# A gated attention and its feed-forward network on one core: the range check of the weights done by VectorE late, instead of by ScalarE throughout

## The chip, the cores and the metric

The kernel runs on one core of a Trainium2 chip. Times are device microseconds (us) of one execution. Five executions of the kernel before took 573.87 to 575.8 us, with a median of 574.09 us. One more execution was recorded by the hardware profiler, and all lines shown from the trace are of that one.

## The reference

Four batches, eight heads, 768 tokens, 48 features a head. A complex gate per token and feature is first brought to a magnitude of at most 0.999; a state is then carried over the tokens, and its real part is read by the queries. The result, 3072 rows of 384, goes through a feed-forward network (FFN):

```
mag = np.sqrt(a_re * a_re + a_im * a_im)
scale = np.minimum(mag, 0.999) / (mag + 1e-06)
...
new_re = ar * S_re - ai * S_im
new_im = ar * S_im + ai * S_re
S_re, S_im = (new_re + kv, new_im)
y[:, :, t] = np.einsum('bhd,bhde->bhe', q[:, :, t], S_re)
...
a = x @ w1
b = x @ w2
h = a * b @ w3
return (h @ w_out).astype(np.float32)
```

w1 and w2 are 384x1024, w3 is 1024x1024, w_out is 1024x384. The four weights arrive as 64-bit floats, all else as 32-bit floats.

## The kernel before, in words

**Work.** The tokens are cut into eight units (u = 0 to 7), two for each batch, of 384 tokens each. For a unit the kernel prepares the gates (`gates(u)`), then does the attention in three chunks of 128 tokens, then the FFN of the unit. The product of w3 and w_out is formed once, at the start (L940), so that an FFN has only two stages. In `ffn_ab` (L714 to L729), for each of eight blocks j of 128 hidden features, TensorE multiplies with w1 and then with w2 into two PSUM buffers (L723), ScalarE copies the first out (L728), and VectorE multiplies the second by that copy (L729, tile `ab`). In `out_pair` and `ffn_out`, TensorE multiplies `ab` by the fused weight (L768, L802). The `mm` PSUM pool has four buffers, so block j+2 can write its second product only when VectorE's product of block j is done.

**Gates.** `gates(u)` is a chain that goes to and fro between ScalarE (logarithm, exponential, arc tangent, sine, all at L544) and VectorE (products and scans, L554 to L620). The gates of unit u+1 are prepared while unit u is worked on. The first TensorE instruction of a unit that needs them is the transpose `tp` of the tile gR (L653); gR is finished by VectorE at L616, tile k at L617.

**The range check.** The kernel's fast way holds only for inputs in a certain range. While it runs, it collects evidence that they are: `check_gates` looks at the gates, and `check_weights` at the weights. Where the evidence is bad, the function `general` computes all again (L1084 to L1086); here it does not. `check_weights` is a generator. Each step loads one piece of a weight (a DMA from SyncE's queue, called SP, into one of two buffers `look`, 512 KB or, for w_out, 384 KB), as pairs of 32-bit words, and looks at the high words of the 64-bit numbers read as 32-bit floats. There are 36 such looks: 28 of 512 numbers a partition, 8 of 384. A look is two ScalarE passes, for the 16 pieces of w3 three: the square of the scaled high word, in place (L885), then Relu with a sum (L886) that is over zero when a number is too small, and for w3 another (L888) that is over zero when one is too large. The sums lie in `st_wts`. `judge` (L946) turns all evidence into counts, adds them over the partitions with one small TensorE product (`count`, L961), and sets the flag `good`. Every engine reads the flag at the end.

**What sets the order.** TensorE's instructions run in the order of the program text (`manual_schedule`, L1009). On the other engines, and in SP's queue, a scheduler orders the instructions when the program is built; `high_priority` lifts some of them, and `follow` (L861) keeps a look behind the last instruction in `copied`. The order is then fixed: each engine, and SP, takes its instructions in turn, and one that waits holds all behind it. `unit` (L993) emits a unit's pieces and takes one look at each of its 10 or 11 places i, for units 2 to 7. After the last unit, the rest of the looks and `judge` are emitted (L1077 to L1079), and then the last FFN, of unit 7, by which the kernel ends.

Of the kernel before, what the change touches and what calls it, by code (L numbers as in the profile page):

```python
# [10 lines left out]
FP = mybir.dt.float32  # L11
I32 = mybir.dt.int32
# [3 lines left out]
AF = mybir.ActivationFunctionType  # L16
# [358 lines left out]
def kernel(  # L375
# [36 lines left out]
    nc = tc.nc  # L412
# [16 lines left out]
    LO, HI = 32, D - 32  # L429
    LN_EPS = math.log(1e-6)  # L430
    PI = math.pi
    MIN_SQ, MAX_SQ = 1.126 ** 2, 2.0 ** 32 - 512
    SMALL, LARGE, STEEP, DECAY, ANGLE = 2.0 ** -7, 2.0 ** 40, 1.5, math.exp(-64.0), 50.0

    weights_pool = ctx.enter_context(tc.tile_pool(name="weights", bufs=1))
# [24 lines left out]
    causal = singles.tile([P, C], I32, name="causal")  # L460
    nc.gpsimd.iota(causal, pattern=[[1, C]], base=0, channel_multiplier=-1)
    nc.vector.tensor_scalar(out=causal, in0=causal, scalar1=0, scalar2=None, op0=OP.is_ge)
    consts = singles.tile([P, 7], FP, name="consts")
    for i, x in enumerate((1.0, LN_EPS, PI / 2, SMALL, -LARGE, MIN_SQ, -MAX_SQ)):
        nc.vector.memset(consts[:, i:i + 1], x)
    ONE, EPS, QUARTER, LEAST, MOST, TINY, TWO = (consts[:, i:i + 1] for i in range(7))

# [2 lines left out]
    nc.vector.memset(st_tan, 0.0)  # L472
    nc.vector.memset(st_low, 0.0)

    st_wts = singles.tile([P, 80], FP, name="st_wts")
    nc.vector.memset(st_wts, 0.0)
    st_dec = singles.tile([P, NU, KD], FP, name="st_dec")
    st_ang = singles.tile([P, NU, KD, UC], FP, name="st_ang")

# [236 lines left out]
    def ffn_ab(u, j):  # L716
        if j == 0:
            ab_t[u] = one.tile([P, KF, TT], FP, tag="ab", name="ab")
        got = []
        for w in (w1s, w2s):  # L720
            m = ps_m.tile([P, TT], FP, tag="mm", name="m")
            for f in range(KD):
                nc.tensor.matmul(out=m, lhsT=w[:, j * P // WB, f, j * P % WB:j * P % WB + P], rhs=xT_t[u][:, f],  # L723
                                 start=(f == 0), stop=(f == KD - 1))
            got.append(m)
        a = two.tile([P, TT], FP, tag="a", name="a")
        with tc.high_priority():
            copied[:] = [nc.scalar.copy(out=a, in_=got[0])]  # L728
            nc.vector.tensor_tensor(out=ab_t[u][:, j], in0=got[1], in1=a, op=OP.mult)  # L729

# [128 lines left out]
    def follow(work):  # L861

        for ins in work:
            tc.add_manual_dep(ins.ins, copied[-1].ins.name, ORDER, reason="later")

    def check_weights(late):

        for u in range(2):
            for f in range(KD):
                re = late.tile([P, 2, TT], FP, tag="look", name="look")  # L870
                load_rows(re, art, u, [f])
                follow(check_gates(u, re[:, 0], re[:, 1], f))
                yield
        n = 0
        for w in (w1, w2, w3t, wo):
            if w.dtype == FP:
                continue
            src = words(w)
            step = min(src.shape[2], 1024)
            for i in range(src.shape[1]):  # L880
                for j in range(0, src.shape[2], step):
                    raw = late.tile([P, 512, 2], I32, tag="look", name="look")
                    nc.sync.dma_start(out=raw[:, 0:step // 2].rearrange("p m w -> p (m w)"), in_=src[:, i, j:j + step])
                    lo, hi = (raw[:, 0:step // 2, x].bitcast(FP) for x in range(2))
                    follow([nc.scalar.activation(out=hi, in_=hi, func=AF.Square, scale=2.0 ** 15)])  # L885
                    nc.scalar.activation(out=lo, in_=hi, func=AF.Relu, scale=-1.0, bias=TINY, accum_out=st_wts[:, n:n + 1])  # L886
                    if w is w3t:
                        nc.scalar.activation(out=hi, in_=hi, func=AF.Relu, bias=TWO, accum_out=st_wts[:, n + 40:n + 41])  # L888
                    n += 1
                    yield  # L890

# [54 lines left out]
    def judge():  # L946

        n = max(NU * KD * UC, st_wts.shape[1])
        ok = singles.tile([P, n], FP, name="ok")
        tot = singles.tile([P, 6], FP, name="tot")  # L950
        dec, ang = st_dec.rearrange("p u f -> p (u f)"), st_ang.rearrange("p u f c -> p (u f c)")
        low, tan = st_low.rearrange("p x u f -> p (x u f)"), st_tan.rearrange("p u f -> p (u f)")
        need = 0
        for i, (t, op, x) in enumerate(((dec, OP.is_ge, DECAY), (ang, OP.is_le, ANGLE), (ang, OP.is_ge, -ANGLE),
                                        (low, OP.is_le, 0.0), (tan, OP.is_le, STEEP * STEEP), (st_wts, OP.is_le, 0.0))):
            m = t.shape[1]
            need += m
            nc.vector.scalar_tensor_tensor(out=ok[:, 0:m], in0=t, scalar=x, in1=ONE.to_broadcast([P, m]), op0=op,
                                           op1=OP.mult, accum_out=tot[:, i:i + 1])
        m = ps_m.tile([P, TT], FP, tag="mm", name="count")  # L960
        nc.tensor.matmul(out=m[0:1, 0:6], lhsT=ONE, rhs=tot, start=True, stop=True)  # L961
        count = singles.tile([1, 7], FP, name="count")
        nc.vector.scalar_tensor_tensor(out=count[:, 0:6], in0=m[0:1, 0:6], scalar=1.0, in1=ONE[0:1].to_broadcast([1, 6]),
                                       op0=OP.mult, op1=OP.mult, accum_out=count[:, 6:7])
        nc.vector.tensor_scalar(out=good, in0=count[:, 6:7], scalar1=float(P * need), scalar2=None, op0=OP.is_equal)

    for A in Ab:
        nc.vector.memset(A, 0.0)
# [24 lines left out]
    def unit(u, steps, rest, look, ahead):  # L993

        for f in rest[:ahead]:
            f()
            next(steps, None)
        rest = rest[ahead:]
        p = pieces(u) + [[]]
        n = len(p)  # L1000
        first = [i * (len(rest) - 2) // (n - 1) for i in range(n)] + [len(rest)] if u > 1 else [0, 1, 1, 2, 2, 3, 3, 3, 4, 4, 6]
        for i in range(n):
            for f in rest[first[i]:first[i + 1]] + p[i]:
                f()
                next(steps, None)
            next(look, None)

    gate_pool[1] = fast.enter_context(tc.tile_pool(name="late_gates", bufs=1))
    with tc.manual_schedule(engines={mybir.EngineType.PE}):  # L1009

        phase = rounding()
        row_load(0, 4)
        load_gates(0)
        row_load(1)
        row_load(2)
        row_load(3)
        take_qk(0)
        steps = gates(0, True)
        for f in range(KF):
            row_work(f)  # L1020
            if f == 0:
                load_qkv(0)
            if f + 4 < KF:
                row_load(f + 4)
            if f >= KF - 2:
                continue
            for j in range(KF):
                fuse(f, j)
            for _ in range(2):
                next(steps, None)  # L1030
        work = w12_work()
        for f in work[:2]:
            f()
        for _ in steps:
            pass
        for f in range(KF - 2, KF):
            for j in range(KF // 2):
                fuse(f, j)
        fill = [lambda f=f, j=j: [fuse(f, j + x) for x in range(2)] for f in range(KF - 2, KF) for j in range(KF // 2, KF, 2)]
        load_gates(1)  # L1040
        steps = gates(1, False)
        take_qk(1)
        rest = ffn(0, 2)
        work = work[2:]
        for i, p in enumerate(pieces(0)):
            for f in p:
                f()
            if i in (1, 3, 6, 9):
                fill.pop(0)()
            if i == 0:  # L1050
                for f in work[:2]:
                    f()
                load_qkv(1)
            if i >= 2:
                next(steps)
            if i in (5, 7):
                work[2 + (i == 7)]()
        for i, f in enumerate(rest[:HEAD]):
            f()
            if i < 2:  # L1060
                work[4 + i]()
            if i == 2:
                phase.close()
            if i < 6:
                next(steps)
            if i == KF - 1:
                for _ in steps:
                    pass
        late = fast.enter_context(tc.tile_pool(name="late", bufs=1))
        look = check_weights(fast.enter_context(tc.tile_pool(name="looks", bufs=2)))  # L1070
        out_weights()
        for u in range(1, NU):
            steps = gates(u + 1, False) if u + 1 < NU else iter(())
            unit(u, steps, rest[HEAD:] if u == 1 else ffn(u - 1), look if u > 1 else iter(()), AHEAD[u])
            for _ in steps:
                pass
        for _ in look:  # L1077
            pass
        judge()  # L1079
        for f in ffn(NU - 1, 2):  # L1080
            f()
    fast.close()

    value = nc.values_load(good[0:1, 0:1], min_val=0, max_val=1)  # L1084
# [38 lines left out]
```

## Time and profile before

| | |
|---|---|
| median of five executions | 574.09 us |
| profiled execution | 573.73 us |
| its span, first to last instruction | 571.8 us |
| mean granted TensorE clock | 0.992 |
| TensorE matmuls (PE) busy | 545.4 us, 95% |
| VectorE (DVE) busy | 335.4 us, 59% |
| ScalarE (ACT) busy | 347.3 us, 61% |
| passes of the looks at the weights on ACT, first and last start | 207.1 and 448.6 us |
| attention of unit 7 and FFN of unit 6 | about 459 to 520 us |
| FFN of unit 7 | 520 us to the end |

The table is read from the top: the span is what the instructions take from first to last, and 1.9 us of the profiled execution lie around it. An engine that is busy 95% of the span leaves little room; engines busy 60% may still be late for it in some places. In a line of the trace, the first number is the start in us from the span's start, or the line group's count where it begins with a source line; "[1.42 <-DVE gR L616]" is idle time before an instruction and the instruction that ended it.

### The profile page before, as it was taken

What the parts mean: (1) busy time and instruction counts of PE and PEld (TensorE: products, weight loads), DVE (VectorE), ACT (ScalarE), POOL (GpSimd) and SP (SyncE); (2) the same over time, 40 slices, a digit from 0 to 9 for tenths busy, and PEclk for the clock granted to TensorE, in tenths of its full rate; (3) what the DMA queues carried; (4) which work ended last, traced back from release to release, by engine and by line L of the source; (5) the groups of instructions that cost most, each with busy time, mean ns of one, the idle gap of its engine ahead of it and who ended that gap; (6) DMA issues with size and microseconds to landing.
All of it is one profiled execution on the core that took longest, in us unless ns stands there. A gap on an engine that the chain in (4) does not pass through costs nothing.

```text
span 571.8 us, 9280 instructions
## 1 busy us (share of the span) xinstructions
PE 545.4 (95%) x3682; PEld 387.2 (68%) x3682; DVE 335.4 (59%) x507; ACT 347.3 (61%) x569; POOL 3.5 (1%) x9
## 2 busy tenths in 40 slices
PE   4779999999999999999999999999999999999995
PEld 2345775578556985688567975697567966796565
DVE  6898489946852577356752686355743696332121
ACT  6998668537572799459963898279964745101100
POOL 2000000000000000000000000000000000000000
PEclk9899999999999999999999999999999999999999
DMA  8994997393273345944593527844483103300001
GB/s 277 368 370 132 251 350 207 111 234 85 86 161 86 112 152 193 240 139 154 182 213 116 150 73 223 214 141 155 130 198 107 30 28 104 76 2 30 0 1 47
DMA packets 46340, 84.74 MB, mean 148 GB/s; under 512 B 4688, under 2 KB 36176, under 8 KB 45392
## 3 DMA queue, kind: packets, MB, share of 16 engines
q1 hardware_dynamic: 46288, 84.06, 50.6%
q8 instruction: 31, 0.51, 0.4%
q14 instruction: 21, 0.17, 0.1%
HBM read 60.42 MB, written 4.72 MB: 114 GB/s over the span
## 4 chain that ended last, share of the span: by engine, by line
PE 66%; DVE 12%; ACT 11%; DMA 6%; issue 3%; SPq 1%; DVEq 0%; ACTq 0%
PE m L723 36%; PE p L768 10%; PE o L802 6%; PE sc L665 4%; PE y L692 4%; PE kv L703 3%; ACT gZ L544 2%; DMA re<-in_a_re_dram 2%; ACT gR L544 2%; DVE gZ L600 2%; PE tp L653 2%; DMA raw<-in_w_dram 2%; DMA QL<-gA 1%; ACT re L544 1%; ACT gA L544 1%
## 5 line engine op out<-in xcount | busy, mean ns | idle before, releaser
L723 PE MATMUL m<-xT,w1s 128*128 128x384 f32 x384 | 135.3, 489 | 1.2 <-ACT xT L694 0.7
L723 PE MATMUL m<-xT,w2s 128*128 128x384 f32 x384 | 134.3, 486 | 0.0
L723 PEld LDWEIGHTS m<-xT,w2s 128*128 128x128 f32 x384 | 73.0, 190 | 50.9
L723 PEld LDWEIGHTS m<-xT,w1s 128*128 128x128 f32 x384 | 71.0, 190 | 47.3 <-ACT xT L694 1.9
L729 DVE TENSOR_TENSOR ab<-m,a 128x384 f32<-128x384 f32 x64 | 35.3, 552 | 84.3 <-PE m L723 76.3
L940 PE MATMUL f<-wo_s,w3s 128*128 128x384 f32 x128 | 49.1, 543 | 15.2 <-DVE wo_s L854 15.2
L728 ACT COPY a<-m 128x384 f32<-128x384 f32 x64 | 30.2, 474 | 49.5 <-PE m L723 48.4
L802 PE MATMUL o<-w3o,ab 128*128 128x384 f32 x160 | 54.0, 487 | 0.0
L655 ACT COPY KT<-tp 128x384 f32<-128x384 f32 x40 | 33.6, 850 | 30.9 <-PE tp L653 30.8
L940 PEld LDWEIGHTS f<-wo_s,w3s 128*128 128x128 f32 x128 | 26.6, 214 | 35.2 <-DVE wo_s L854 17.1
L665 PE MATMUL sc<-QL,KL 96*128 96x128 f32 x384 | 47.2, 276 | 0.6 <-DVE A L667 0.5
L665 PEld LDWEIGHTS sc<-QL,KL 96*128 96x128 f32 x384 | 45.7, 192 | 1.7 <-DVE A L667 0.7
L710 DVE TENSOR_TENSOR T<-kv,T 96x512 f32<-96x512 f32 x16 | 11.0, 687 | 54.5 <-PE kv L703 54.5
L667 DVE COPY_PREDICATED A<-causal,sc 128x512 f32<-128x512 int32 x48 | 34.4, 738 | 14.0 <-PE sc L665 13.3
L802 PEld LDWEIGHTS o<-w3o,ab 128*128 128x128 f32 x160 | 29.6, 190 | 18.7 <-issue 0.4
L692 PE MATMUL y<-A,V 128*32 128x128 f32 x768 | 39.3, 275 | 0.0
L692 PEld LDWEIGHTS y<-A,V 128*32 128x32 f32 x768 | 32.9, 109 | 3.5 <-issue 1.3
L692 PE MATMUL y<-QL,T 96*32 96x128 f32 x640 | 34.6, 272 | 0.0
L768 PE MATMUL p<-To,So 128*128 128x192 f32 x168 | 31.6, 335 | 0.1
L703 PEld LDWEIGHTS kv<-V,KT 128*96 128x96 f32 x320 | 29.6, 165 | 3.0 <-issue 1.3
L544 ACT ACTIVATE re<-gZ 128x1152 int32<-128x1152 f32 (+3 forms) x20 | 19.1, 966 | 20.3 <-DVE gZ L600 15.3
L692 PEld LDWEIGHTS y<-QL,T 96*32 96x32 f32 x640 | 31.3, 110 | 0.0
(113 smaller groups left out, 753.8 us busy)
## 6 DMA issues: line engine op xcount, KB each, us to landing
look<-in_w_dram SPq DMA_DIRECT2D x28, 512.0 KB, 3.7
raw<-in_w_dram SPq DMA_DIRECT2D x7, 1024.0 KB, 10.9
raw<-in_w_dram SPq DMA_DIRECT2D x8, 768.0 KB, 8.1
KL<-gR SPq DMA_DIRECT2D x24, 192.5 KB, 3.6
KL<-k SPq DMA_DIRECT2D x24, 192.5 KB, 4.0
re<-in_a_re_dram SPq DMA_DIRECT2D x24, 192.0 KB, 5.2
im<-in_a_im_dram SPq DMA_DIRECT2D x24, 192.0 KB, 3.2
k<-in_k_dram SPq DMA_DIRECT2D x24, 192.0 KB, 4.0
```

Source lines behind the costliest of these rows:

```text
L544: chain(nc.scalar.activation(**kw))
L655: nc.scalar.copy(out=KT_t[u, c][:, :, :, x].rearrange("p h d f -> p f d h"), in_=tp.rearrange("p f (d h) -> p f d h", h=H))
L665: nc.tensor.matmul(out=sc[:, j], lhsT=KL[:, x * n + j, w], rhs=QL[:, x * n + j, w], start=True, stop=True)
L667: nc.vector.copy_predicated(out=A[:, x * n:(x + 1) * n], data=sc, mask=causal.rearrange("p (h t) -> p h t", h=1).to_broadcast([P, n, C]))
L692: nc.tensor.matmul(out=o, lhsT=a, rhs=b, start=s0, stop=s1)
L703: nc.tensor.matmul(out=kv[:, hd], lhsT=KT[:, hd].rearrange("p d x f -> p (d x f)"), rhs=V[:, hd], start=True, stop=True)
L723: nc.tensor.matmul(out=m, lhsT=w[:, j * P // WB, f, j * P % WB:j * P % WB + P], rhs=xT_t[u][:, f], start=(f == 0), stop=(f == KD - 1))
L728: copied[:] = [nc.scalar.copy(out=a, in_=got[0])]
L729: nc.vector.tensor_tensor(out=ab_t[u][:, j], in0=got[1], in1=a, op=OP.mult)
L768: nc.tensor.matmul(out=m[p], lhsT=a[:, f], rhs=b[:, f], start=(f == 0), stop=(f == KH - 1))
L802: nc.tensor.matmul(out=m, lhsT=ab_t[u][:, f, t * P:(t + 1) * P], rhs=w3o[:, f], start=(f == 0), stop=(f == KF - 1))
L940: nc.tensor.matmul(out=sums[j], lhsT=w3_t[f][:, j * P:(j + 1) * P], rhs=w3_t["wo"][:, f], start=(f == 0), stop=(f == KF - 1))
```

## The change

The looks at the weights move from ScalarE to VectorE, and most of them to later. A look is now three VectorE instructions: the sign bit is taken off the high words, in place; they are clamped to the range, into the low words' place; and the clamped words are compared with the unclamped, the equal ones counted (512 or 384 a look and partition). `unit` takes a look at every place only in units 6 and 7, in units 2 to 5 at each fourth place; the rest, two after each piece, and then `judge`, are emitted within the last FFN, `judge` after its ninth piece, the first half of `ffn_out`. `copied` now holds VectorE's product instead of ScalarE's copy. The loads, their sizes and the two buffers stay.

```
-            copied[:] = [nc.scalar.copy(out=a, in_=got[0])]
-            nc.vector.tensor_tensor(out=ab_t[u][:, j], in0=got[1], in1=a, op=OP.mult)
+            nc.scalar.copy(out=a, in_=got[0])
+            copied[:] = [nc.vector.tensor_tensor(out=ab_t[u][:, j], in0=got[1], in1=a, op=OP.mult)]
...
-                    follow([nc.scalar.activation(out=hi, in_=hi, func=AF.Square, scale=2.0 ** 15)])
-                    nc.scalar.activation(out=lo, in_=hi, func=AF.Relu, scale=-1.0, bias=TINY, accum_out=st_wts[:, n:n + 1])
-                    if w is w3t:
-                        nc.scalar.activation(out=hi, in_=hi, func=AF.Relu, bias=TWO, accum_out=st_wts[:, n + 40:n + 41])
+                    follow([nc.vector.tensor_scalar(out=hi.bitcast(I32), in0=hi.bitcast(I32), scalar1=0x7FFFFFFF,
+                                                    scalar2=None, op0=OP.bitwise_and)])
+                    nc.vector.tensor_scalar(out=lo, in0=hi, scalar1=MIN_HI, scalar2=MAX_HI if w is w3t else 3.0e38, op0=OP.max,
+                                            op1=OP.min)
+                    nc.vector.scalar_tensor_tensor(out=lo, in0=hi, scalar=1.0, in1=lo, op0=OP.mult, op1=OP.is_equal,
+                                                   accum_out=st_wts[:, n:n + 1])
...
-            next(look, None)
+            if u > NU - 3 or i % 4 == 0:
+                next(look, None)
...
-        for _ in look:
-            pass
-        judge()
-        for f in ffn(NU - 1, 2):
+        for i, f in enumerate(ffn(NU - 1, 2)):
             f()
+            for _ in range(2):
+                next(look, None)
+            if i == KF:
+                for _ in look:
+                    pass
+                judge()
```

The rest of the diff fits the buffers of counts (`st_wts` has 36 columns instead of 80, `judge` makes seven counts instead of six) and drops two constants.

More of the change, by code (lines that the diff above doesn't have):

```diff
@@ L431 @@
     PI = math.pi
-    MIN_SQ, MAX_SQ = 1.126 ** 2, 2.0 ** 32 - 512
+    MIN_HI, MAX_HI = 1.126 * 2.0 ** -15, 2.0 - 2.0 ** -23
     SMALL, LARGE, STEEP, DECAY, ANGLE = 2.0 ** -7, 2.0 ** 40, 1.5, math.exp(-64.0), 50.0
@@ L462 @@
     nc.vector.tensor_scalar(out=causal, in0=causal, scalar1=0, scalar2=None, op0=OP.is_ge)
-    consts = singles.tile([P, 7], FP, name="consts")
-    for i, x in enumerate((1.0, LN_EPS, PI / 2, SMALL, -LARGE, MIN_SQ, -MAX_SQ)):
+    consts = singles.tile([P, 5], FP, name="consts")
+    for i, x in enumerate((1.0, LN_EPS, PI / 2, SMALL, -LARGE)):
         nc.vector.memset(consts[:, i:i + 1], x)
-    ONE, EPS, QUARTER, LEAST, MOST, TINY, TWO = (consts[:, i:i + 1] for i in range(7))
+    ONE, EPS, QUARTER, LEAST, MOST = (consts[:, i:i + 1] for i in range(5))
     st_tan = singles.tile([P, NU, KD], FP, name="st_tan")
@@ L473 @@
     nc.vector.memset(st_low, 0.0)
-    st_wts = singles.tile([P, 80], FP, name="st_wts")
-    nc.vector.memset(st_wts, 0.0)
+    WTS = 28
+    st_wts = singles.tile([P, WTS + KF], FP, name="st_wts")
+    nc.vector.memset(st_wts[:, 0:WTS], 512.0)
+    nc.vector.memset(st_wts[:, WTS:], DM)
     st_dec = singles.tile([P, NU, KD], FP, name="st_dec")
@@ L879, in check_weights @@
             step = min(src.shape[2], 1024)
+            if w is wo:
+                n = WTS
             for i in range(src.shape[1]):
@@ L949, in judge @@
         ok = singles.tile([P, n], FP, name="ok")
-        tot = singles.tile([P, 6], FP, name="tot")
+        tot = singles.tile([P, 7], FP, name="tot")
         dec, ang = st_dec.rearrange("p u f -> p (u f)"), st_ang.rearrange("p u f c -> p (u f c)")
@@ L954, in judge @@
         for i, (t, op, x) in enumerate(((dec, OP.is_ge, DECAY), (ang, OP.is_le, ANGLE), (ang, OP.is_ge, -ANGLE),
-                                        (low, OP.is_le, 0.0), (tan, OP.is_le, STEEP * STEEP), (st_wts, OP.is_le, 0.0))):
+                                        (low, OP.is_le, 0.0), (tan, OP.is_le, STEEP * STEEP), (st_wts[:, 0:WTS], OP.is_ge, 512.0),
+                                        (st_wts[:, WTS:], OP.is_ge, float(DM)))):
             m = t.shape[1]
@@ L960, in judge @@
         m = ps_m.tile([P, TT], FP, tag="mm", name="count")
[L961 to L965, printed above, removed]
+        nc.tensor.matmul(out=m[0:1, 0:7], lhsT=ONE, rhs=tot, start=True, stop=True)
+        count = singles.tile([1, 8], FP, name="count")
+        nc.vector.scalar_tensor_tensor(out=count[:, 0:7], in0=m[0:1, 0:7], scalar=1.0, in1=ONE[0:1].to_broadcast([1, 7]),
+                                       op0=OP.mult, op1=OP.mult, accum_out=count[:, 7:8])
+        nc.vector.tensor_scalar(out=good, in0=count[:, 7:8], scalar1=float(P * need), scalar2=None, op0=OP.is_equal)
     for A in Ab:
```

## The prediction, made before the changed kernel ran

> **What bounds the kernel now.** I read the page's shares of the span first, then the stages, then TensorE's waits.
>
> ```profile
> PE 545.4 (95%) x3682; PEld 387.2 (68%) x3682; DVE 335.4 (59%) x507; ACT 347.3 (61%) x569; POOL 3.5 (1%) x9
> ```
>
> ```profile
> 380.00:400.00 20.00, 19.81 (x265) 16.45 (x257) 12.92 (x20) 18.72 (x36) 0.00 (x0) 1.00 0.44 136
> 400.00:420.00 20.00, 18.58 (x62) 10.79 (x61) 15.93 (x18) 18.94 (x36) 0.00 (x0) 1.00 0.47 140
> ```
>
> In the stages of 20 us the columns are length, then busy time (and count) of PE, PEld, DVE, ACT, POOL, then clock and DMA. From 160 us, where the first looks run, to 560 us PE is idle 2.4 us in all, and 1.42 of them fall between 400 and 420, where ACT is 95% busy. So TensorE sets the end, and a change on other engines can win these 2.4 us and no more, but can lose without limit. The timeline shows the 1.42:
>
> ```profile
> 414.11 1.36 DVE L616 TENSOR_TENSOR gR<-k,re 128x1152 f32<-128x1152 f32 x1 [0.60 <-ACT re L544]
> ```
>
> ```profile
> 415.62 0.52 PE L653 MATMUL tp<-ident,gR 128*128 128x128 f32 x3 [1.42 <-DVE gR L616]
> ```
>
> PE reached unit 6's first transpose before that unit's gates were done. The same place in unit 7 was met: gR ended at 477.54 (476.18 + 1.36), PE came at 478.10, 0.56 us later.
>
> **What goes.** These are the looks, by tile:
>
> ```profile
> L885 ACT ACTIVATE look<-look x36: 545/679/733, 207.1 to 448.0; 128x512 f32<-128x512 f32 x28, 128x384 f32<-128x384 f32 x8
> L886 ACT ACTIVATE look<-look,consts x36: 640/770/793, 208.1 to 448.6; 128x512 f32<-128x512 f32 x28, 128x384 f32<-128x384 f32 x8
> L888 ACT ACTIVATE look<-look,consts x16: 762/778/811, 281.4 to 403.8; 128x512 f32<-128x512 f32 x16
> DMA to landing us min/median/max: 2.9/3.6/7.5
> ```
>
> With the reads of their sums (52 of 0.19) ACT loses 23.2 + 26.8 + 12.4 + 10.0 = 72.4 us. Between 375 and 414 us, while unit 6's gates ran, 23 such passes and 14 reads took about 17 us of ACT. In the changed program's order one VectorE look (1.6 us, below) stands in that chain instead. The chain was 1.42 us late, so that wait goes: **-1.4 us**. Next late is nothing but TensorE: k (L617) was ready at 417.34 and read at 419.85.
>
> **What comes: one look.** By form of the rows: a one-source DVE operation that reads every second word, as a look does, took 549 ns for 768 numbers and 354 for 384 (L844), so 0.42 us for 512. L586, two sources, took 1355 for 1152 and 554 for 384, so 0.69 for 512. The same kind of operation with a sum:
>
> ```profile
> L958 DVE SCALAR_TENSOR_TENSOR ok<-st_wts,consts x1: 241/241/241, 472.1 to 472.1; 128x80 f32<-128x80 f32 x1
> ```
>
> It lies on L586's line, (554 - 384 x 1.04) + 80 x 1.04 = 238 ns: the sum costs nothing in the stream. A look is 0.42 + 0.42 + 0.69, plus 0.03 after each since they depend on each other (the adds at L756: 0.36 long, 0.39 apart): 1.6 us, of 384 numbers 1.35. In all DVE gains 28 x 1.53 + 8 x 1.26 = 53 us.
>
> No row writes every second word on DVE. The nearest are on ACT: L885 takes 0.688 for 512, while dense L544 rows (516 for 384, 1159 for 1152) give 0.623, 10% less. So a look may cost 0.15 more. Upper bounds: sign and clamp at the two-source rate, 0.69 each (+0.54 a look); the count at the rate of the slowest two-source row, the scan L576 (943 ns for 384, 1.22 for 512; +0.53). Below: the dense rates; no row of such a form and size is faster, so there is no gain to bound. I take dense plus 10%, because L844 and L850 (686 ns for 1024) show alternate words read at no loss.
>
> [...]
>
> **Where they come.** In the changed order 8 looks fall into units 2 to 5, where DVE is idle for 3 to 13 us of each 20, one look to a gate chain at most, and I find no product L729 pushed past the time PE needs its buffer: nothing. Seven fall into unit 6, eight into unit 7, thirteen into the last FFN.
>
> *Unit 6, gates of unit 7.* Between im (L554, 447.21) and L616 (476.18) now stand five signs, five clamps and four counts: 10 x 0.42 + 4 x 0.69 = 7.0 us. DVE was idle there for 1.15 + 1.70 + 0.96 + 2.05 = 5.9 us. And the chain starts earlier: ACT's exponential gR waited from 441.59 to 443.74 behind looks, so im moves to about 445.7, a gain of 1.5. 7.0 - 5.9 - 1.5 = -0.4: with the 0.56 of slack a margin of 1.0 us. **0**; at +0.27 for each sign and clamp, 2.7 - 1.0 = +1.7; at the slow count, 4 x 0.53 - 1.0 = +1.1. The products L729 queued behind looks come 1 to 2 us later; PE needs the tightest (ended 474.1) at 476.17.
>
> *Unit 7 and the last FFN.* Two buffers feed the looks, and DVE waits for each transfer at the head of its queue, the product L729 behind it. From issue to use it took 3.6 us:
>
> ```profile
> 381.37 7.46 SPq L883 DMA_DIRECT2D look<-in_w_dram  x3
> ```
>
> ```profile
> 384.98 0.73 ACT L885 ACTIVATE look<-look 128x512 f32<-128x512 f32 x1 [0.51 <-DMA look<-in_w_dram]
> ```
>
> For 384 numbers 3.0 (the one issued at 443.23). So a buffer turns in 3.6 + 1.6 = 5.2 us, or 3.0 + 1.35 = 4.35, and two looks take a turn. From look 18, whose buffer comes free at about 502.7 (after the first scores of unit 7), 11 looks of 512 and 8 of 384 need 5.5 x 5.2 + 4 x 4.35 = 46.0 us: 548.7. DVE's other work in that stretch is 4 copies x 0.73, 7 adds x 0.36, 7 products x 0.55, 0.95 of sums and evidence, 10.2 us; most falls into the waits for transfers (5.2 - 3.2 = 2.0 a turn). All hidden gives 548.7, none 558.9. Laid row by row in the changed order, 3.7 are not hidden: 552.4. The limit is new: PE's `count` product stands after the first half of `ffn_out`, which ended at 553.56, and needs the last look. Behind it on PE are the last products; behind the flag in SP's queue the last three outputs, not due before 564. Margin 1.2 us; with 10% a look, 9.5 x 0.15 = 1.4 is used: **+0.2**. The products are 2 to 3 us late by then, of the 5.8 they have (two blocks less the half that does not need them). Copies of the scores and adds have 2 us and more.
>
> **Sum.** Against the profiled execution, 573.73: -1.4 + 0 + 0.2 = 572.5. The median of the runs is 0.36 above that one; I give **572.9**, 0.2% less, within no change. Below 0.3%, 1.7 us, this kernel's measurement cannot tell it from no change.
>
> **Rivals.**
> 1. *All hidden*: no surcharge, and the small waits go too (2.36 idle, less 0.41 behind L776 in the last FFN): 574.09 - 1.95 = 572.1. For it: ACT's 72 us. Against: beside the 1.42 the trace names ACT for one of these waits only (xT, 0.2). Faster by over 0.3%: 0.20.
> 2. *Forecast*, 572.4 to 575.8: 0.42.
> 3. *The turn of the two buffers bounds the last FFN* (slower). Place: look 18 to `count`. It decides from 0.13 us more a turn; then each 0.1 us in a look or a landing costs 0.95. Signs and clamps at 0.69: 5.5 x 0.54 + 4 x 0.40 - 1.2 = +3.4, and 1.7 in unit 6: 574.09 - 1.4 + 5.1 = 577.8. The slow count: +3.3 and 1.1: 577.1. Landings of 4.0: 9.5 x 0.4 - 1.2 = +2.6: 575.3, so it takes 0.45 more to pass the bound. Both slow: 584. For it: the margin is a fortieth of the stretch, and every unknown lengthens. Against: the rows of L844 and L958. 0.36.
> 4. *The change does not reach the wait at 415*: the chain there was slow by itself, 574: 0.02, as ACT was busy 37.7 of 40 us.
>
> Faster 0.20, same 0.44, slower 0.36. The range, 571.9 to 578.5, ends 0.2 below rival 1 and above either single slow rate; both slow (about 0.1) is left out.
>
> **What would show it.** Right: ACT near 275 us, DVE near 390; no PE wait at unit 6's tp; sign and clamp 0.42 to 0.46, count 0.69 to 0.76; `count` starting at once after L802's first half. Wrong: PE waiting in L723 for L729 or at `count` (rival 3), at unit 7's tp (the margin of 1.0), or transfers over 3.7 us.

## The result, and the profile after

The changed kernel takes 576.47 us (median of 35 runs, 573.99 to 579.26) where the kernel before takes 574.67 (60 runs): ratio 1.0029, with a 95% interval of 1.002 to 1.0038. It is slower by 0.3%, 1.7 us. The forecast was 572.9.

The profiled execution of the changed kernel took 578.25 us (span 576.5), 1.8 above its own median, so its waits are at the long end, and sizes are taken from the experiments. Line numbers are two higher than before up to the looks. First the page's shares, as before:

```profile
PE 545.7 (95%) x3682; PEld 387.2 (67%) x3682; DVE 382.1 (66%) x652; ACT 290.5 (50%) x429; POOL 3.5 (1%) x9
```

ACT lost 57 us and DVE gained 47; PE has the same 546 us of work in a span that is 4.7 us longer. The stages of 20 us show where PE idles now (length, then busy time and count of PE, PEld, DVE, ACT, POOL, then clock and DMA):

```profile
260.00:280.00 20.00, 17.36 (x190) 13.47 (x190) 14.85 (x21) 12.67 (x19) 0.00 (x0) 1.00 0.18 51
...
380.00:400.00 20.00, 18.48 (x272) 16.39 (x271) 14.98 (x24) 11.06 (x16) 0.00 (x0) 1.00 0.33 106
400.00:420.00 20.00, 20.00 (x66) 11.87 (x65) 16.72 (x22) 11.98 (x15) 0.00 (x0) 1.00 0.42 106
...
500.00:520.00 20.00, 19.11 (x294) 17.98 (x292) 14.23 (x33) 2.05 (x5) 0.00 (x0) 1.00 0.45 142
520.00:540.00 20.00, 19.41 (x67) 12.31 (x68) 13.41 (x37) 1.92 (x4) 0.00 (x0) 1.00 0.63 196
```

From 400 to 420, where PE was idle 1.42 before, it is now busy throughout. But 2.6 us are idle in 260 to 280 (0.1 before), 1.5 in 380 to 400 (0.2 before), and 1.5 in 500 to 540 (none before). The wait that the change was to meet is gone, by the timeline of VectorE and of TensorE:

```profile
411.69 1.36 DVE L618 TENSOR_TENSOR gR<-k,re 128x1152 f32<-128x1152 f32 x1 [2.05 <-ACT re L546]
```

```profile
417.69 0.49 PE L655 MATMUL tp<-ident,gR 128*128 128x128 f32 x3
```

gR ended at 413.05, and PE reached its transpose at 417.69 without waiting. What PE waits for instead, in its timeline:

```profile
269.42 1.57 PE L770 MATMUL p<-To,So 128*128 128x192 f32 x8 [1.97 <-DVE U L758]
272.96 2.20 PE L725 MATMUL m<-xT,w1s 128*128 128x384 f32 x6 [0.67 <-ACT xT L696]
...
394.69 1.57 PE L770 MATMUL p<-To,So 128*128 128x192 f32 x8 [0.85 <-DVE U L758]
...
520.42 1.57 PE L770 MATMUL p<-To,So 128*128 128x192 f32 x8 [1.31 <-DVE U L758]
537.01 2.20 PE L725 MATMUL m<-xT,w2s 128*128 128x384 f32 x6 [0.17 <-DVE ab L731]
557.79 0.19 PE L969 MATMUL count<-tot,consts 128*1 128x7 f32 x2 [0.52 <-DVE ok L966]
```

L758 are the adds of `out_pair`, short VectorE instructions (0.35 us) that empty the PSUM buffers of the FFN's output products L770. They were late three times, in units 3, 5 and 7. They are not slow; they stand in VectorE's queue behind something that is. In unit 7 it is a look:

```profile
517.73 0.43 DVE L889 TENSOR_SCALAR look<-look 128x512 int32<-128x512 int32 x1 [1.47 <-DMA look<-in_w_dram]
518.19 0.51 DVE L892 TENSOR_SCALAR look<-look 128x512 f32<-128x512 f32 x1
518.74 0.69 DVE L894 SCALAR_TENSOR_TENSOR look<-look 128x512 f32<-128x512 f32 x1
519.36 0.08 DVE L894 DVE_READ_ACCUMULATOR look<-look 128x1 f32 x1
519.36 0.35 DVE L758 TENSOR_TENSOR U<-p,ot 128x192 f32<-128x192 f32 x1
```

VectorE waited 1.47 us for the look's transfer, worked 1.6 on the look, and only then came to the add for which TensorE stood. In unit 5 a look stands the same way ahead of the gate chain (it waits 0.94 for its transfer at 385.77), and the adds stand behind the chain. In unit 3 it is ScalarE that waits, in a place that the diff does not show:

```profile
253.15 0.60 SPq L487 DMA_DIRECT2D look<-in_a_re_dram  x1
253.79 7.07 SPq L887 DMA_DIRECT2D look<-in_w_dram  x2
...
259.03 0.61 ACT L521 ACTIVATE look<-look,consts 128x384 f32<-128x384 f32 x1 [3.28 <-DMA look<-in_a_re_dram]
...
266.97 0.76 DVE L576 TENSOR_SCALAR gA<-gA 128x1152 f32<-128x1152 f32 x1 [2.31 <-ACT gA L546]
267.64 0.35 DVE L758 TENSOR_TENSOR U<-p,ot 128x192 f32<-128x192 f32 x1
```

The look at 259.03 is not at a weight but at the gates' input a_re. The generator's first six steps are such gate looks. At the old pace all six fell into unit 2; at each fourth place the last comes in unit 3. Its transfer is issued 0.6 us ahead of a weight piece of 512 KB and reaches its reader 5.9 us later. (The second of the two weight issues in that line ends at 253.79 + 7.07 = 260.86, after the gate look is done and its buffer free: only one is behind the gate look's transfer.) ScalarE waits for the gate look with the gate chain behind, VectorE's step L576 waits for the chain, and the add waits behind L576.

### The profile page after: what moved, and what is told of

Read it like the earlier page. It is cut to its first block, busy times and chain, and to the rows that moved or that the text cites. A ratio compares the mean times of both kernels' runs of the same rounds, so it can differ in the third digit from the quotient of the medians.

```text
span 576.5 us, 9279 instructions
## 1 busy us (share of the span) xinstructions
PE 545.7 (95%) x3682; PEld 387.2 (67%) x3682; DVE 382.1 (66%) x652; ACT 290.5 (50%) x429; POOL 3.5 (1%) x9
## 4 chain that ended last, share of the span: by engine, by line
PE 59%; DVE 15%; DMA 12%; ACT 7%; issue 4%; SPq 2%; ACTq 0%; DVEq 0%
PE m L725 34%; PE p L770 7%; PE o L804 6%; DMA look<-in_w_dram 5%; PE kv L705 3%; PE sc L667 3%; PE y L694 3%; ACT gZ L546 2%; DMA look<-in_w_out_dram 2%; DMA re<-in_a_re_dram 2%; PE tp L655 2%; DMA QL<-gA 1%; DVE gZ L602 1%; PE f L947 1%; ACT gR L546 1%
## 5 line engine op out<-in xcount | busy, mean ns | idle before, releaser
L712 DVE TENSOR_TENSOR T<-kv,T 96x512 f32<-96x512 f32 x16 | 11.0, 687 | 52.7 <-PE kv L705 52.7
L770 PE MATMUL p<-To,So 128*128 128x192 f32 x168 | 31.6, 335 | 4.1 <-DVE U L758 4.1
L770 PEld LDWEIGHTS p<-To,So 128*128 128x128 f32 x168 | 27.0, 190 | 7.6 <-DVE U L758 4.9
```

What stands on the lines that cost most here:

```text
L770: nc.tensor.matmul(out=m[p], lhsT=a[:, f], rhs=b[:, f], start=(f == 0), stop=(f == KH - 1))
```

## The experiments

Each run is told with its ratio to the kernel before on the same chip (on the four chips of the experiments its median was 574.52 to 574.83); 0.001 is 0.57 us. Where a run leaves work out, its expectation says which.

**e1, the gate looks early.** Theory A: the gate looks' pace is the cause. Theory B: the turn of the two look buffers late in the kernel is.

```diff
-            if u > NU - 3 or i % 4 == 0:
+            if u > NU - 3 or u > 3 and i % 4 == 0 or u == 2 and i < 6:
```

> The six looks at the gates' inputs (a_re, on ScalarE) are again taken at unit 2's first six places, as in the kernel before; the looks at the weights stay as the change has them. Theory A (the slower pace also moved the gate looks, the last of them into unit 3, where its late transfer holds ScalarE's queue, the gate chain behind it, and the adds behind the chain): the 2.6 us in which TensorE idles between 260 and 280 us fall to 0.1, and the time falls by 1.5 to 2.6 against the changed kernel, to 574.0 to 575.0, within 0.2% of the kernel before. What idles after 380 us (about 1.5 in unit 5 and 1.5 to 2 from 500 on) stays. Theory B (the turn of the two look buffers in unit 7 and the last FFN costs nearly all): TensorE's idle time in unit 3 was peculiar to the one profiled execution or is made up for later; the time stays within 0.5 of the changed kernel.

576.15 us, ratio 1.0025 (1.0011 to 1.0039). In its trace the 2.6 us in unit 3 are 0.44, as theory A had it, but the time is only 0.0004 lower than the changed kernel's (0.0021 lower than in its second measurement, below): adds waited 0.49 in unit 5 and 1.69 in unit 7. A is not the main cause.

**e2 and e3, half pieces in four buffers** (e3 with the edit of e1 as well).

```diff
-                    raw = late.tile([P, 512, 2], I32, tag="look", name="look")
+                        raw = late.tile([P, 256, 2], I32, tag="look", name="look")
...
-                    n += 1
-                    yield
+                        n += 1
+                        if n % 2 == 0:
+                            yield
...
-        look = check_weights(fast.enter_context(tc.tile_pool(name="looks", bufs=2)))
+        look = check_weights()
```

(`check_weights` opens the four buffers itself, once the gate looks have given up theirs.)

> The changed kernel with the weights' looks in pieces of half the size (256 numbers instead of 512, 192 instead of 384), two pieces a step, and four buffers in place of two in the same room; pace and gate looks stay. Three more fixed costs on VectorE for each extra piece, some 36 x 0.2 = 7 us in all. Theory A (gate looks): the idle time of 2.6 us in 260 to 280 stays; the adds and the count product after 500 us wait less, since two transfers are under way while two pieces are worked on: time lower than the changed kernel by 0.5 to 1.5. Theory B (turn of the buffers): landings of the smaller pieces are 2.5 to 3 us instead of 4 to 5, no wait of TensorE behind the adds, the products and the count after 500 us, and the time falls by 2 to 3.5 against the changed kernel, below the kernel before.

> Both edits: gate looks early, and four buffers of half pieces. Theory A and B both let all the new waits go except the one in unit 5 (1.5 us in the profiled execution, where a look stands ahead of the gate chain): before less 1.4 for unit 6's first transpose, plus 0 to 1.5: 573 to 574.5. If it is slower than the kernel before, neither theory has the cause, and VectorE's own work (47 us more) is what costs.

e2: 579.17, ratio 1.0066 (1.0041 to 1.0092). e3: 578.76, ratio 1.0073 (1.0045 to 1.0101). Both are slower than the change itself, against both theories: more buffers are no cure. TensorE's timeline of e2 shows one wait of 4 us:

```profile
519.32 2.93 PE L770 MATMUL p<-To,So 128*128 128x192 f32 x8 [3.99 <-DVE U L758]
```

VectorE's timeline shows what it waited for:

```profile
516.38 0.35 DVE L758 TENSOR_TENSOR U<-p,ot 128x192 f32<-128x192 f32 x1
...
518.36 0.30 DVE L891 TENSOR_SCALAR look<-look 128x256 int32<-128x256 int32 x1 [0.96 <-DMA look<-in_w_dram]
...
518.91 0.35 DVE L758 TENSOR_TENSOR U<-p,U 128x192 f32<-128x192 f32 x1
```

Half looks now stand between the adds as well, and one waits for its transfer there. So it is not the number of buffers that decides, but what stands where in VectorE's queue.

**e4, no looks at the weights**, and **e7, the kernel before without them**: what there is to win, and whether the new pace of the gate looks costs by itself.

```diff
-        for w in (w1, w2, w3t, wo):
+        for w in ():
```

> The changed kernel without any look at the weights (it leaves out that part of the check); the gate looks keep the changed pace. Theory A (gate looks): TensorE's idle 2.6 us in 260 to 280 stays, all the others go and so does the wait of 1.4 at unit 6's first transpose: the kernel before plus 0.5 to 1.0, that is 575.0 to 575.7. Theory B (the buffers' turn): the time is that of the kernel before less 1.4 to 1.9, near 572.9, since nothing is left that turns.

> The kernel before without any look at the weights (the weights' check is left out). Both theories: the wait of 1.42 us at unit 6's first transpose goes and little else: 1.3 to 1.9 below the kernel before, 572.6 to 573.2, the same as the changed kernel without looks (573.1). If it is lower than that by over 0.5, the gate looks' pace costs by itself; if it is within 0.5 of the kernel before, ScalarE's looks had no part in the wait at 415 us.

e4: 573.09, ratio 0.9968 (0.9956 to 0.9979). e7: 573.11, ratio 0.9977 (0.9961 to 0.9993). By the ratios, ScalarE's looks cost the kernel before 1.3 to 1.8 us, about the wait of 1.42 at unit 6's transpose, and that is all there is to win. Of this the traces show only half: the wait is gone in both, but each has two waits of about 0.5 behind xT, where the kernel before has one of 0.19. Where the rest comes from stays open. e4 has the gate look in unit 3 too, and loses nothing by it. ACT's timeline of e4:

```profile
257.63 0.62 ACT L521 ACTIVATE look<-look,consts 128x384 f32<-128x384 f32 x1 [1.10 <-DMA look<-in_a_re_dram]
```

Its transfer was issued at 253.92 and took 3.7 us, with no weight piece behind it, against 5.9. So the pace alone does no harm; with a weight piece issued right behind the gate look's transfer it does. Theory A falls as it was put.

**e8, the late looks without the early eight.** (Of these, six are emitted in units 2 to 5 and two at unit 6's first places; on VectorE they start between 294 and 423 us.)

```diff
+                    if w is w1 and (i * src.shape[2] + j) // step < 8:
+                        n += 1
+                        yield
+                        continue
```

> The changed kernel with the first eight looks at the weights, those of units 2 to 5, left out (that part of the weights' check is not made); the 28 of units 6, 7 and the last FFN stay at their places. Theory C (the sparse looks of units 2 to 5 cost: one's transfer delays a gate look's in unit 3, one stands ahead of unit 5's gate chain): the time falls by 1.5 to 3 against the changed kernel, to 573.5 to 575, and no wait of TensorE over 0.5 us is left before 480 us. Theory B (the dense stretch from unit 7 on costs, where two buffers feed VectorE and it waits for transfers at the head of its queue): the time stays within 0.7 of the changed kernel's 576.5, and 1.5 to 2.5 us above the kernel without looks (573.1) lie in TensorE's waits after 500 us.

576.9, ratio 1.0037 (1.0019 to 1.0054): nothing is won by leaving the early eight out. But this run was not clean: the first of the late pieces, whose buffer was free, was again issued right behind the gate look's transfer (at 253.41), and the adds at 268.46 waited 1.38 us.

**e13, the late looks alone**, with the gate looks early and no transfer of a look in units 3 to 5.

```diff
+                    if w is w1 and (i * src.shape[2] + j) // step < 8:
+                        n += 1
+                        continue
...
-            if u > NU - 3 or i % 4 == 0:
+            if u > NU - 3 or u == 2 and i < 6:
```

> The changed kernel with the gate looks at unit 2's first six places, the first eight looks at the weights left out (that part of the check is not made) and nothing of the looks, transfers neither, in units 3 to 5; what is left are the 28 looks of units 6, 7 and the last FFN. Theory B (they stand in VectorE's queue ahead of the adds, masks and products, and wait there for their transfers): 575.0 to 576.5, that is 2 to 3 above the kernel without looks (573.1) and 0.3 to 1 below the changed kernel. Theory C (the early eight and the gate looks' pace carry the loss): 573.0 to 573.8.

575.25, ratio 1.0009 (0.9996 to 1.0021), 2.2 us above e4: theory B. Its trace shows PE waiting, besides the 0.41 at 557.26 that all these kernels have, at four places after 500 us (its lines are three higher from the looks on):

```profile
517.03 1.57 PE L770 MATMUL p<-To,So 128*128 128x192 f32 x8 [1.14 <-DVE U L758]
533.72 2.20 PE L725 MATMUL m<-xT,w2s 128*128 128x384 f32 x6 [0.27 <-DVE ab L731]
541.99 2.20 PE L725 MATMUL m<-xT,w2s 128*128 128x384 f32 x6 [0.19 <-DVE ab L731]
555.16 0.19 PE L972 MATMUL count<-tot,consts 128*1 128x7 f32 x2 [0.65 <-DVE ok L969]
```

The sum is 2.25 us; by the ratios it is 0.0041 above e4, 2.4 us. Half of the waiting is met at the adds, over a quarter at `count`. But that is where PE first meets the delay, not what sets its size. In the changed kernel's trace, the chain of work that ended last runs from 520.75 us on from look to transfer to look, up to `count`:

```profile
528.25 4.62 DMA look<-in_w_dram
...
532.90 0.44 DVE look L889
...
553.13 3.02 DMA look<-in_w_out_dram
...
556.96 0.58 DVE look L894 x2
...
557.79 0.19 PE count L969 x2
```

`count` waits in each of the five traces with the same late looks (0.52 to 0.71: e1, e8, e13, the changed kernel twice). So an add that came earlier would bring PE to `count` earlier, to wait there for the same last look: the length of this chain decides. That is read from the traces; no run moved the adds alone.

**e14, the early looks alone**, and **the changed kernel once more**.

```diff
+                    if n == 8:
+                        return
```

> The changed kernel with only its first eight looks at the weights, those of units 2 to 5, and the gate looks at its slow pace; the other 28 are left out (that part of the check is not made). Theory G (the parts add up: 0.6 us more than no looks before unit 6, 2.2 from unit 6 on, the sum of what the other runs leave): 573.1 without looks plus 1.2, so 574.0 to 574.8, and in its trace a wait of TensorE behind the adds at 269 us and one at 395. Theory H (these waits are given back later, or were peculiar to one execution): 572.8 to 573.5.

> The changed kernel itself, for a second trace on the same chip as the two others. Theory G: 576 to 577 and the waits of the first trace again, behind the adds in unit 3 or 5 and in unit 7, and at the count product, in sum 3 to 5 us. Theory H: the waits before 400 us are absent from this trace.

e14: 574.34, ratio 0.9998 (0.9978 to 1.0017), 0.0030 or 1.7 us above e4. Its waits are those of the changed kernel, shorter, in units 3 and 5:

```profile
267.74 1.57 PE L770 MATMUL p<-To,So 128*128 128x192 f32 x8 [1.03 <-DVE U L758]
...
392.89 1.57 PE L770 MATMUL p<-To,So 128*128 128x192 f32 x8 [0.72 <-DVE U L758]
```

The second trace of the changed kernel (ratio 1.0046, 1.0029 to 1.0064) has the waits of the first again: 2.90 and 0.30 behind the adds of units 3 and 5, 1.37 in unit 7, 0.72 behind a product, 0.56 at `count`. Theory G holds: the parts add up. Relative to before: -0.0032 without looks, +0.0030 for the early, +0.0041 for the late ones, together +0.0039, and 1.0029 to 1.0046 was measured; each part is known to 0.001 or 0.002 only. How the 1.7 us divide between units 3 and 5 stays open: the three traces differ, and e1, which took away unit 3's part, won 0.2 us against the one measurement of the changed kernel and 1.2 against the other.

**e9, VectorE's looks without transfers.**

```diff
-                    raw = late.tile([P, 512, 2], I32, tag="look", name="look")
-                    nc.sync.dma_start(out=raw[:, 0:step // 2].rearrange("p m w -> p (m w)"), in_=src[:, i, j:j + step])
+                    if n == 0:
+                        raw = late.tile([P, 512, 2], I32, tag="look", name="look")
+                        nc.vector.memset(raw.bitcast(FP), 1.0)
```

> The changed kernel with VectorE's 36 looks at their places, all at one tile that is filled once, so without the looks' 36 transfers (it leaves out the weights' check, since no weights are looked at). Theory B (VectorE waits for the transfers at the head of its queue): the time is that of the kernel without looks, 573.0 to 573.8, though VectorE works 50 us more than there, and TensorE's waits behind the adds and at the count product are gone. Theory E (VectorE's own work, 1.6 us a look, is in the way wherever it stands): 575 or more, half of the loss or more stays.

583.1, ratio 1.0151 (1.0128 to 1.0174), the slowest of all, against theory B's 573.0 to 573.8. It is no clean test, for without the transfers the order that was built is another: it has the looks together, six of them from 433.8 to 445.4 us ahead of two masks of unit 6's scores. VectorE at the end of these six:

```profile
443.86 0.43 DVE L890 TENSOR_SCALAR look<-look 128x512 int32<-128x512 int32 x1
...
444.79 0.69 DVE L895 SCALAR_TENSOR_TENSOR look<-look 128x512 f32<-128x512 f32 x1
445.40 0.08 DVE L895 DVE_READ_ACCUMULATOR look<-look 128x1 f32 x1
445.40 1.33 DVE L669 COPY_PREDICATED A<-causal,sc 128x512 f32<-128x512 int32 x2
```

and TensorE, which waits for the masks (and again, 3.49, for those of unit 7):

```profile
446.18 2.05 PE L667 MATMUL sc<-QL,KL 96*128 96x128 f32 x16 [2.70 <-DVE A L669]
```

So it does not take a transfer: a look costs when urgent work stands behind it in the queue, whether it waits or works.

**e10, early looks at other places.**

```diff
-            if u > NU - 3 or i % 4 == 0:
+            if u > NU - 3 or u == 2 or i >= 5:
```

> The changed kernel with another pace: in unit 2 a look at every place (the six gate looks as in the kernel before), in units 3 to 5 a look at each place from the sixth on, in units 6 and 7 one at every place as before; so about 17 looks at the weights before unit 6 in place of 8, nearly all done before the last FFN. Theory B (density from unit 7 on): 573.0 to 574.0, below the kernel before, since what remains after unit 7 is a few looks. Theory C (looks among the gate chains cost): the early stalls grow instead, one for each unit's chain that gets looks, 1 to 1.5 us each in units 3, 4 and 5: 575 to 577. Where both act the total is near the changed kernel's and the place of TensorE's waits tells.

579.14, ratio 1.0068 (1.0044 to 1.0092). TensorE's timeline shows theory C: 2.32 at unit 3's transpose and 2.05 and 1.74 behind the adds. After 500 us nothing is left but the 0.41:

```profile
230.26 0.52 PE L655 MATMUL tp<-ident,gR 128*128 128x128 f32 x3 [2.32 <-DVE gR L618]
...
273.00 1.57 PE L770 MATMUL p<-To,So 128*128 128x192 f32 x8 [2.05 <-DVE U L758]
...
398.45 1.57 PE L770 MATMUL p<-To,So 128*128 128x192 f32 x8 [1.74 <-DVE U L758]
```

The places from the sixth on were thought idle; they are where the next unit's gate chain runs.

**e5 and e6, the halves of the change**: the engine without the place, and the place without the engine.

```diff
-            if u > NU - 3 or i % 4 == 0:
-                next(look, None)
+            next(look, None)
...
+        for _ in look:
+            pass
+        judge()
```

> Half of the change: VectorE's looks, but at the pace of the kernel before (one at every place from unit 2 on, the rest and the judgement ahead of the last FFN). Theory B in its narrow form (only the density from unit 7 on costs): 573.0 to 574.0, as nearly all looks are done by unit 6. Theory F (a look costs wherever it stands in VectorE's queue ahead of a gate chain, of masks or of adds, since it waits there for its transfer): like the kernel with the idle places, 578 to 580, or more, with TensorE's waits behind gR at the first transposes of units 3 to 6 and behind the adds; none after 500 us.

(e6 has L885 to L888 of the kernel before, and the pace and tail of the changed one.)

> The other half of the change: ScalarE's passes, at the places and the pace of the changed kernel (sparse in units 2 to 5, dense in units 6, 7 and the last FFN). Theory B and F: no masks, adds or products of VectorE stand behind the looks any more, but a turn of the two buffers is 0.4 to 1 us longer (two to three passes of 0.64 to 0.77 and their reads against 1.6), and the products' copies stand behind passes: TensorE waits for ScalarE's copies in the last FFN and for the count product, 576 to 580. If only VectorE's queue matters and ScalarE has room: 573.5 to 574.5, below the kernel before.

e5: 577.47, ratio 1.0051 (1.0034 to 1.0068). e6: 580.13, ratio 1.0096 (1.0075 to 1.0117). e6 is slower than both halves together; e5 is slower than the kernel before, but not clear of the changed kernel (1.0029 and 1.0046). In e5, VectorE's looks among the gate chains make the first transposes of units 3 and 7 late (1.90 and 1.63); theory F had expected that in units 3 to 6, with waits behind the adds too, and 578 or more. In e6 the adds of units 3 and 5 wait 1.15 and 2.06, and the copy xT that the last FFN begins with stands behind ScalarE's passes, one of which waits for its transfer:

```profile
526.70 2.20 PE L723 MATMUL m<-xT,w1s 128*128 128x384 f32 x6 [2.85 <-ACT xT L694]
```

**e12 and e15, both engines, each where its queue has room.** ScalarE's passes for the first 26 looks (e15: 20), in units 2 to 4; VectorE's for the rest.

```diff
+                    if n < FIRST:
+                        first = nc.scalar.activation(out=hi, in_=hi, func=AF.Square, scale=2.0 ** 15)
...
-            if u > NU - 3 or i % 4 == 0:
+            if u < 5 or u == 6 and i < 2 or u == NU - 1:
```

(In e15 the pace is: u < 4, or u == 4 and i < 5, or u in (5, 6) and i < 2, or u == NU - 1 and i % 2 == 0. In both the last FFN takes one look a piece.)

> A candidate that looks at all weights: ScalarE's passes at every place of units 2 to 4 (26 looks, as in the kernel before, which lost nothing to them before 375 us), none in unit 5 whose chain was late, and VectorE's looks for the other ten, two after unit 6's gate chain and the rest at unit 7's places, where VectorE idles. Theory F: 572.8 to 573.6, the time without looks, 0.2% below the kernel before; no wait at unit 6's first transpose, none behind adds or masks. If VectorE's looks cost wherever they are, 574 or more.

> The kernel with both engines, with ScalarE's looks ending three to six places earlier (20 instead of 26) so that none is left at the head of unit 6's gate chain, and VectorE's 16 spread: two right after each of the chains of units 6 and 7 (where its queue holds only products), five at every second place of unit 7, seven in the last FFN, one behind each product. Theory F (the place in the queue decides): no wait at unit 6's first transpose, none behind adds or masks, 572.5 to 573.3. If VectorE's looks in the last FFN cost by themselves: 574 to 575, with TensorE waiting behind the products or at the count.

e12: 573.28, ratio 0.9978 (0.9967 to 0.9988). e15: 573.31, ratio 0.9978 (0.9966 to 0.9989). Both look at all weights and beat the kernel before by 0.2% and the changed one by 0.5%; they are within 0.001 of having no looks at all. So VectorE's looks cost next to nothing where no add, mask or chain stands behind them. (They also have fewer looks late, so the chain of transfers up to `count` is shorter.) Neither is as expected throughout: both have a wait of 0.4 to 0.5 behind the adds of unit 3. e12's trace still has 1.26 at unit 6's transpose; ScalarE's looks reach into that chain until 391 us, where e15's end before it. One trace does not show where e12's gain of 1.3 us is. e15's trace has no wait there, but a look that waits for its transfer ahead of a mask of unit 7:

```profile
502.73 1.16 PE L669 MATMUL sc<-QL,KL 96*128 96x128 f32 x8 [1.21 <-DVE A L671]
```

## Why the prediction was wrong, point by point

- **"That wait goes: -1.4 us": right.** The transpose at 417.69 waits for nothing; e4 gives 1.8, e7 1.3 for having no looks, of which the traces show half.
- **One look, 1.6 us: right.** The looks in the changed kernel, by tile:

```profile
L889 DVE TENSOR_SCALAR look<-look x36: 360/418/441, 293.8 to 556.2; 128x512 int32<-128x512 int32 x28, 128x384 int32<-128x384 int32 x8
L892 DVE TENSOR_SCALAR look<-look x36: 357/426/514, 294.2 to 556.6; 128x512 f32<-128x512 f32 x28, 128x384 f32<-128x384 f32 x8
L894 DVE SCALAR_TENSOR_TENSOR look<-look x36: 550/692/708, 294.7 to 557.0; 128x512 f32<-128x512 f32 x28, 128x384 f32<-128x384 f32 x8
```

  These are the dense rates of 0.42, 0.42 and 0.69; the 10% that were added for writing every second word are not there. With two 32-bit sources and a sum the count took 0.69 us for 512, where the upper bound from the scan was 1.22.
- **"ACT near 275 us, DVE near 390": wrong.** ACT was busy 290.5 and DVE 382.1. The lengths of the rows were added up, but neighbours overlap by about 0.1 us on ACT (a pass of 1.17 that starts at 251.06 is followed at 252.13): leaving out looks of 72.4 us took 56.5 off ACT's busy time (e7: 290.8). Nothing in the sum rests on it.
- **"Units 2 to 5: nothing": wrong, +1.7 us (e14).** "No product L729 pushed past the time PE needs its buffer" was true and not enough. The adds L758 behind the looks and behind the chain were not followed, and that the gate looks share the generator, so that the pace moves them and their transfers too, was not seen.
- **Unit 6, the gates of unit 7, "0": right.** gR ended at 478.27 (476.92 + 1.35), PE took it at 480.14 without waiting.
- **Unit 7 and the last FFN, "+0.2": wrong, +2.4 us (e13).** The path was right: the two buffers' turn up to `count`. Its size was not. A landing of 3.6 us was too short: the 11 of 512 numbers took 3.6 to 5.2, median 4.3 (over the whole kernel the median went from 3.7 to 4.7). So two looks turned in 5.9 us instead of 5.2 (11 looks from 508.80 to 538.14), and the stretch took 52.7 (from 504.74, the issue of the first, to 557.44) where 49.7 had been laid out, and 51.1 with the 10%; the margin was 1.2. The seven transfers of looks issued from 423 to 476 us took 3.5 to 7.0, median 4.8, and PE lost 0.08 in all from 400 to 500: a long landing costs where much has to be done by a fixed point, or something urgent stands behind it. "Copies of the scores and adds have 2 us and more" was wrong as well: the add at 519.36 stood behind a late look and made PE wait 1.31, ahead of the 0.52 at `count`.
- **Rival 3** had the mechanism of the late part. For landings of 4.0 in all turns it gave 575.3, and the late looks alone took 575.25. The landings were 4.3 for 512 numbers and 3.0, as laid out, for 384, which by its rule is about the same: 5.5 x 0.7 - 1.2 = 2.7. The 1.7 us of units 2 to 5 it did not have.
- **The sum.** 572.9, plus 1.7 for units 2 to 5, plus 2.2 more for the late stage, is 576.8; 576.5 was measured.

## What to carry to other kernels

An engine that is idle two thirds of a stage (VectorE before the change from 500 to 520 us: busy 6.57 of 20) still has a queue in a fixed order: before moving work there, list what stands behind each moved instruction, and who waits for that, the shortest instructions too. Follow every step of a generator whose pace is changed, with its transfers, not the steps that the change is about alone. Where a row of transfers and looks has to be through by a fixed point, its length decides, wherever the waits show first (here 52.7 us up to `count`, where 51.1 had been laid out); price it with the landings that it will have itself. Here the same check cost from 0.1% to 1.3% over no check (e15, e6: 0.9978 and 1.0096 against 0.9968), by its engine and place: put it right after the last urgent instruction of a chain, not ahead of the next.

## What the runs showed of the hardware

- A transfer of 192 KB issued behind the same loads of k and q reached its reader after 3.7 us with nothing behind it (e4), and after 4.9 (e14), 5.3 (e8), 5.9 and 6.8 us (the changed kernel's two traces) with one of 512 KB issued 0.6 us behind it: what is issued later slowed what was issued first.
- Pieces of half the bytes did not land in half the time: 3.7 us (median) for 256 KB in e2, with four buffers, against 4.7 for 512 KB in the changed kernel, with two. On VectorE half the numbers took 0.28, 0.29 and 0.42 us against 0.42, 0.43 and 0.69.
- Reading a sum back took VectorE 0.08 us, and the next instruction started with it (both at 519.36); ScalarE's read took 0.19.
